# Gate sums on VectorE, denominators packed and their reciprocals spread by DMA, and the attention state folded into the output weights on 16 tiles of 32x32

## The chip, the core and the metric

The kernel runs on one core of a Trainium2 chip. The metric is the device time of one execution in microseconds (us). The core has a matrix engine (TensorE, "PE" in the profile; its weight loads are "PEld"), VectorE (DVE), ScalarE (ACT), GpSimd (POOL) and SyncE (SP), which here issues nearly all DMAs. In the traces here each engine works through its own queue in the order in which the kernel wrote it, and engines wait for each other on semaphores.

All runs below are of the same state (fast, granted TensorE clock 0.996 to 1.000). The runs came in five groups, each in turn on one chip, and the kernel before stood in each; its median moved between groups by 0.1 us only.

## The reference, cut to what matters

For `x` of 2048 tokens by 1024, two attention blocks with 32 heads of 32 are mixed by a gate. Block A is linear attention, block B a sliding window (not touched by the change, apart from its place in the schedule).

```python
g = sigmoid((x * gate_w).sum(-1, keepdims=True))
# block A
phi = lambda t: where(t > 0, t + 1, exp(t)) + 1e-6
pq, pk = phi(q), phi(k)
kv  = einsum("bhsd,bhse->bhde", pk, v)          # the state, 32x32 a head
z   = pk.sum over tokens                         # 32 numbers a head
den = einsum("bhqd,bhd->bhq", pq, z) + 1e-6      # one number a head and token
a   = ((pq @ kv) / den) @ A_wo
return g * a + (1 - g) * b
```

Both kernels fold the state into the weights: `(pq/den) @ (kv @ A_wo)`. So three small products stand beside the large ones: the gate sums, the denominators, and the fold of `kv` into `A_wo`.

## The kernel before: the parts that matter here

The kernel is written as a list of operations with costs. A scheduler inside it runs that list through a simple model of the engines ("the plan") and so fixes each engine's order; it then emits waits for what each operation reads.

The gate, on TensorE, with the sums on four column tiles, then a trip through DRAM to turn the layout:

```python
for dc in range(8):
    for u in range(4):
        last = e.matmul(gbank.ap()[32*u:32*u+32, :], gwr[:, dc, :], xT[:, dc, u*512:(u+1)*512],
                        start=(dc == 0), stop=(dc == 7), tile_position=(0, 32*u), ...)
P.op("act", lambda e: e.activation(gts[:, :], gbank.ap(), ACT.Exp, scale=-1.0), ...)
... # store gts, load it back transposed, 1/(1+.)
```

The state is placed as four 32x32 blocks on the diagonal of eight 128x128 matrices (`kvbd`), turned by TensorE, and folded with full matmuls; `zbd` repeats `z` so that a full matmul gives the denominator in every row of its head:

```python
def fold(i, jh):       # 16 of these
    P.op("pe", lambda e: e.matmul(bank.ap(), kvT[:, i, :], ws[1][:, i, jh*512:(jh+1)*512], start=True, stop=True), ...)
    move(ws[1][:, i, jh*512:(jh+1)*512], bank.ap, 512, bank, w)

def numer(u, j):       # 32 of these: queries of heads 4j..4j+3, tokens 512u..512u+511
    group(bank, w, xs, [wr, xr])                       # 8 full matmuls
    phi(bank, p_, preg, 8*u + j)                       # Exp on ACT, two operations on DVE
    def over():
        P.op("pe", lambda e: e.matmul(db.ap(), zbd[:, j, :], p_, start=True, stop=True), ..., name="den")
        P.op("act", ... R = Ln(den + eps))
        P.op("act", ... R = Exp(-R))                   # the reciprocal
        P.op("dve", lambda e: e.tensor_tensor(dst, p_, R[:, :], ALU.mult), ...)
    after(6 if u == 0 else 2, over)
```

The end of the program: all engines read a flag (whether the fast path's range assumptions held) and jump over a slower general path, which in all these runs is not taken. SyncE first waits for every DMA semaphore that the kernel used:

```python
def tail(e, eng):
    e.wait_ge(*flag_op.val)
    e.reg_load(reg, flag[0:1, 0:1])
    if eng == "sp":
        for s, v in P.final:              # one entry for each DMA semaphore
            e.wait_ge(s, v)
    with e.If_eq(reg, 0):
        ... # the general path
```

## Time and profile before

501.64 us, median of 3 runs (501.62 to 503.03).

| engine | busy, us | share of the span |
|---|---|---|
| PE | 493.2 | 99% |
| DVE | 267.6 | 54% |
| ACT | 191.4 | 38% |

From the profile page of the kernel before. In a group's line the columns are: source line, engine, operation, output and input tiles, shapes, count, busy us in total and mean ns of one, then the engine's idle time just ahead of them.

```profile
span 500.1 us, 11359 instructions
PE 493.2 (99%) x5113; PEld 231.4 (46%) x5113; DVE 267.6 (54%) x460; ACT 191.4 (38%) x331; POOL 6.6 (1%) x30
PE 96%; SPq 2%; DMA 1%; ACT 1%; issue 0%; DVE 0%
L1325 PE MATMUL ps_all<-w,xT 128*128 128x512 bf16 x960 | 214.2, 379 | 1.1 <-DMA xT<-in_A_x_dram 0.9
L1607 ACT ACTIVATE ra<-ps_all,eps 128x512 f32<-128x512 f32 x32 | 21.5, 689 | 2.1 <-PE ps_all L1605 2.0
```

The third line is the chain of work that ended last: 96% of it is TensorE. The 379 ns of one matmul is not what it costs, because matmuls overlap; the cost shows in the chain. From the chain of waits of the kernel before, in order of time (start us, us, what):

```profile
62.08 1.84 PE ps_all L1393 x32
128.55 5.29 PE ps_all L1325 x24
325.53 0.45 PE ps_all L1573 x8
327.70 0.86 PE ps_all L1583 x4
330.30 0.22 PE ps_all L1605
342.42 0.69 ACT ra L1607
343.11 0.58 ACT e L1334 x2
343.69 0.52 ACT ra L1608
344.20 1.17 ACT ra L1607 x2
```

Full matmuls (L1325) cost 5.29 / 24 = 0.22 us each, or 0.216 in long runs. L1393 is the gate, L1573 the turn, L1583 the fold, L1605 a denominator. The last four lines are the one place where TensorE depends on ACT.

### The profile page before, as it was taken

What the parts mean: (1) busy time and instruction counts of PE and PEld (TensorE: products, weight loads), DVE (VectorE), ACT (ScalarE), POOL (GpSimd) and SP (SyncE); (2) the same over time, 40 slices, a digit from 0 to 9 for tenths busy, and PEclk for the clock granted to TensorE, in tenths of its full rate; (3) what the DMA queues carried; (4) which work ended last, traced back from release to release, by engine and by line L of the source; (5) the groups of instructions that cost most, each with busy time, mean ns of one, the idle gap of its engine ahead of it and who ended that gap; (6) DMA issues with size and microseconds to landing.
All of it is one profiled execution on the core that took longest, in us unless ns stands there. A gap on an engine that the chain in (4) does not pass through costs nothing.

```text
span 500.1 us, 11359 instructions
## 1 busy us (share of the span) xinstructions
PE 493.2 (99%) x5113; PEld 231.4 (46%) x5113; DVE 267.6 (54%) x460; ACT 191.4 (38%) x331; POOL 6.6 (1%) x30
## 2 busy tenths in 40 slices
PE   8999999999999999999999999999999999999996
PEld 3444444444444445554545454444444444444443
DVE  3112136555676785665556564678776663234443
ACT  1111111111334345656655555489955543200000
POOL 5000000000000000000000000000000000000000
PEclk9999999999999999999999999999999999999999
DMA  8999990000023151011010000500000000011222
GB/s 230 202 209 312 344 283 1 1 0 1 12 90 125 32 182 34 24 42 26 27 43 24 24 1 3 171 0 1 0 2 0 1 1 0 3 43 64 84 85 67
DMA packets 47410, 34.91 MB, mean 70 GB/s; under 512 B 22261, under 2 KB 43125, under 8 KB 47354
## 3 DMA queue, kind: packets, MB, share of 16 engines
q1 hardware_dynamic: 46810, 33.59, 23.6%
q8 instruction: 42, 0.69, 0.6%
q10 hardware_dynamic: 544, 0.52, 0.4%
q14 instruction: 14, 0.11, 0.1%
HBM read 21.51 MB, written 8.40 MB: 60 GB/s over the span
## 4 chain that ended last, share of the span: by engine, by line
PE 96%; SPq 2%; DMA 1%; ACT 1%; issue 0%; DVE 0%
PE ps_all L1325 76%; PE ps_all L1680 11%; PE ps_all L1428 2%; PE ps_all L1447 2%; PE ps_all L1605 1%; SPq L1295 1%; PE ps_all L1526 1%; DMA w<-in_B_wqkv_dram 1%; PE ps_all L1454 1%; PE ps_all L1583 1%; SPq L1300 1%; ACT ra L1607 0%; PE ps_all L1393 0%; ACT e L1334 0%; ACT ra L1608 0%
## 5 line engine op out<-in xcount | busy, mean ns | idle before, releaser
L1325 PE MATMUL ps_all<-w,xT 128*128 128x512 bf16 x960 | 214.2, 379 | 1.1 <-DMA xT<-in_A_x_dram 0.9
L1325 PE MATMUL ps_all<-xT,w 128*128 128x512 bf16 x768 | 172.1, 379 | 0.1
L1325 PEld LDWEIGHTS ps_all<-w,xT 128*128 128x128 bf16 x960 | 91.1, 98 | 109.9 <-DMA w<-in_B_wqkv_dram 1.4
L1325 PEld LDWEIGHTS ps_all<-xT,w 128*128 128x128 bf16 x768 | 74.1, 98 | 88.8 <-ACT ra L1607 0.6
L1680 PE MATMUL ps_all<-w,qT 128*128 128x512 bf16 (+1 forms) x264 | 55.4, 373 | 0.0
L1680 PEld LDWEIGHTS ps_all<-w,qT 128*128 128x128 bf16 x264 | 25.8, 98 | 29.7
L1336 DVE TENSOR_SCALAR e<-e 128x512 bf16<-128x512 bf16 x64 | 18.4, 291 | 30.9 <-ACT e L1332 17.1
L1434 ACT ACTIVATE E<-ps_all 128x1824 bf16<-128x1824 f32 (+1 forms) x18 | 30.4, 1688 | 11.7 <-PE ps_all L1428 10.9
L1356 DVE CAST vst<-ps_all 128x512 bf16<-128x512 f32 x15 | 10.4, 692 | 42.7 <-PE ps_all L1325 42.7
L1437 DVE TENSOR_TENSOR E<-E,msk 128x1824 bf16<-128x1824 bf16 (+1 forms) x18 | 19.8, 1102 | 22.2 <-ACT E L1434 22.2
L1684 DVE SCALAR_TENSOR_TENSOR o<-ps_all,gm,xT 128x512 bf16<-128x512 f32 (+1 forms) x25 | 18.2, 729 | 23.0 <-PE ps_all L1680 22.8
L1334 ACT ACTIVATE e<-ps_all 128x512 bf16<-128x512 f32 x32 | 19.2, 601 | 27.5 <-PE ps_all L1325 26.0
L1332 ACT ACTIVATE e<-ps_all 128x512 bf16<-128x512 f32 x32 | 19.1, 598 | 26.7 <-PE ps_all L1325 25.8
L1281 DVE TENSOR_TENSOR mx<-mx,qT 128x1024 bf16<-128x1024 bf16 x32 | 20.7, 688 | 15.3 <-ACT qT L1360 15.2
L1281 DVE TENSOR_TENSOR mx<-mx,kT 128x1024 bf16<-128x1024 bf16 x32 | 20.7, 688 | 14.8 <-ACT kT L1357 14.7
L1357 ACT ACTIVATE vst<-ps_all 128x512 bf16<-128x512 f32 x17 | 10.2, 597 | 47.8 <-PE ps_all L1325 47.8
L1466 DVE TENSOR_TENSOR qT<-ps_all,L 128x456 bf16<-128x456 f32 (+1 forms) x36 | 21.0, 627 | 6.2 <-ACT L L1464 5.0
L1463 ACT ACTIVATE L<-ps_all 128x456 f32<-128x456 f32 (+1 forms) x36 | 17.8, 547 | 12.4 <-PE ps_all L1447 12.4
L1607 ACT ACTIVATE ra<-ps_all,eps 128x512 f32<-128x512 f32 x32 | 21.5, 689 | 2.1 <-PE ps_all L1605 2.0
L1338 DVE SCALAR_TENSOR_TENSOR pk<-ps_all,e 128x512 bf16<-128x512 f32 x32 | 21.9, 688 | 0.7
L1359 DVE TENSOR_SCALAR xT<-ps_all,g 128x512 bf16<-128x512 f32 x15 | 11.2, 750 | 19.9 <-PE ps_all L1325 19.9
L1360 ACT ACTIVATE qT<-ps_all 128x512 bf16<-128x512 f32 x14 | 8.4, 597 | 34.4 <-PE ps_all L1325 34.4
(77 smaller groups left out, 321.2 us busy)
## 6 DMA issues: line engine op xcount, KB each, us to landing
w<-in_A_wqkv_dram SPq DMA_DIRECT2D x6, 1024.0 KB, 7.0
v<-vB_hbm SPq DMA_DIRECT2D x36, 128.0 KB, 2.6
vB_hbm<-vst SPq DMA_DIRECT2D x32, 128.0 KB, 4.7
w<-in_B_wqkv_dram SPq DMA_DIRECT2D x4, 1024.0 KB, 8.4
out_dram<-o SPq DMA_DIRECT2D x15, 256.0 KB, 2.0
w<-in_A_wo_dram SPq DMA_DIRECT2D x2, 1024.0 KB, 5.2
w<-in_B_wo_dram SPq DMA_DIRECT2D x2, 1024.0 KB, 6.7
w<-in_B_wqkv_dram SPq DMA_DIRECT2D x6, 256.0 KB, 4.3
```

What stands on the lines that cost most here:

```text
L1281: P.op("dve", lambda e, m=m, op=op: e.tensor_tensor(m[:, 0:n], m[:, 0:n], src, op), 0.08 + n / 1920.0, reads=[m.all(), reg], writes=[m.all()],
L1325: last = e.matmul(bank.ap(), lhs(dc), rhs(dc), start=(dc == 0), stop=(dc == 7))
L1332: P.op("act", lambda e: e.activation(e_[:, :], bank.ap(), ACT.Exp), act(512), reads=[bank.iv], writes=[e_.all()])
L1334: P.op("act", lambda e: e.activation(e_[:, :], bank.ap(), ACT.Exp, accum_out=qe[:, col:col + 1]), act(512) + 0.1, reads=[bank.iv], writes= ...
L1336: P.op("dve", lambda e: e.tensor_scalar(e_[:, :], e_[:, :], 1.0, 1e-6, op0=ALU.min, op1=ALU.add), 0.25, reads=[e_.all()], writes=[e_.all()])
L1338: P.op("dve", lambda e: e.scalar_tensor_tensor(out=dst, in0=bank.ap(), scalar=0.0, in1=e_[:, :], op0=ALU.max, op1=ALU.add), dps(512), read ...
L1434: P.op("act", lambda e: e.activation(E[:, 0:32 * nq].rearrange("p (j q) -> p j q", j=4), ps[:, 4:8, 0:8 * nq], ACT.Exp), act(32 * nq), rea ...
L1437: P.op("dve", lambda e: e.tensor_tensor(ev(), ev(), m[:, :, :].rearrange("p r q -> p (r q)")[:, None, :].to_broadcast([128, 16, 2 * nq]), ...
L1466: P.op("dve", lambda e, L=L, h=h, q0=q0: e.tensor_tensor(qT[:, :, q0:q0 + nq], SO[h].ap(0, n).rearrange("p (c q) -> p c q", c=8), L[:, 0:n ...
L1607: P.op("act", lambda e: e.activation(R[:, :], db.ap(), ACT.Ln, bias=eps[:, :]), act(512), reads=[db.iv, eps.all()], writes=[R.all()])
L1680: last = e.matmul(bank.ap(0, f1 - f0), qT[:, dc, t * 128:(t + 1) * 128], ws[3][:, dc, f0:f1], start=(dc == 0), stop=(dc == 7))
L1684: P.op("dve", lambda e, bank=bank, o_=o_, t=t, n=n, i0=i0, i1=i1, tgt=tgt, c0=c0: e.scalar_tensor_tensor(out=o_[:, i0 * 128:i1 * 128].rear ...
```

## The change

Its intent is to take small work off TensorE, which bounds the kernel.

1. The gate's sums move to VectorE: x is loaded a second time in natural order, and one operation for each of 16 token tiles multiplies and sums.
2. The denominators of 8 head groups are made together: 8 matmuls on four column tiles ("a pack"), 4 packs in all. Each head's denominator is made once instead of in 32 rows, its reciprocal is taken once, and DMAs spread it over the rows (store to DRAM, load with a repeated row). The 32 reciprocal pairs on ACT become 4.
3. The fold runs as 4 packs of 16 matmuls of 32x32, four output banks each. The heads are laid out anew, so that a 32x32 transpose by VectorE replaces TensorE's turn.
4. Three output tiles of block B are moved ahead of the last part of block A, to cover the last spread.

The diff, cut to its core (the head layout, tile allocation and the moved final loop are left out):

```diff
-        P.op("pe", gate_fn, 1.75, mode="c", reads=[gwr.all(), xT.all()], writes=[gbank.iv], name="gate")
... (store and load of the gate)
+        for t in range(NT):
+            xt, xs_ = xn.next()
+            P.op("sp", lambda e, t=t, xt=xt: e.dma_start(xt[:, :], x2[t // 8, (t % 8) * 128:(t % 8) * 128 + 128, :]), ...)
+            P.op("dve", lambda e, t=t, xt=xt: e.scalar_tensor_tensor(out=xt[:, :], in0=xt[:, :], scalar=1.0, in1=gwb[:, :],
+                                                    op0=ALU.mult, op1=ALU.mult, accum_out=gt[:, t:t + 1]), ...)
... (fold)
-            P.op("pe", lambda e: e.matmul(bank.ap(), kvT[:, i, :], ws[1][:, i, jh * 512:(jh + 1) * 512], ...), name="fold")
+                for r in range(4):
+                    for c in range(4):
+                        sl = 4 * I + r
+                        last = e.matmul(four[c].ap()[32 * r:32 * r + 32, :], kvT[32 * c:32 * c + 32, 32 * sl:32 * sl + 32],
+                                        ws[1][32 * c:32 * c + 32, sl, jh * 512:(jh + 1) * 512], tile_position=(32 * c, 32 * r), ...)
... (denominators: now one call for each u, three slots after the last numerator of u)
+        def over(u):
+                for q in range(2):
+                    for c in range(4):
+                        last = e.matmul(db.ap()[32 * c:32 * c + 32, :], zsel[:, 2 * c + q, :], tgt[:, 2 * c + q, c0:c0 + 512],
+                                        start=(q == 0), stop=(q == 1), tile_position=(0, 32 * c), ...)
... (R = Exp(-Ln(den + eps)) on ACT as before)
+            for c in range(4):
+                P.op("sp", ... e.dma_start(rc_hbm[u, 8 * c:8 * c + 8, :, :], R[32 * c:32 * c + 8, None, :].to_broadcast([8, 4, 512])), ...
+                     chan="rco%d_%d" % (rs, c), lat=0.5)
+            for j in range(8):
+                B, bs = RBr.next()
+                src = rc_hbm[u, 4 * j:4 * j + 4, :, :].rearrange("r k n -> (r k) n")[:, None, :].to_broadcast([16, 8, 512])
+                P.op("sp", ... e.dma_start(B[:, :], src), ..., chan="rci%d" % bs, lat=1.0)
+                P.op("dve", ... e.tensor_tensor(dst, dst, B[:, :], ALU.mult), ...)
```

## The prediction

> **What bounds the kernel now.** TensorE, from about 8 us to 496 us. The page gives PE 99% of a 500.1 us span; the chain of waits is 96% PE; PE's list of waits has only start-up (1.3 us warm tile, 0.9 us xT); the granted clock is 1.00 in every stage window. In the chain 8 full matmuls (128x128 weights, 512 columns) cost 1.73 us, 0.216 us each. DVE is 54% and ACT 38% busy and matter only where they hold PSUM banks: in the numerator-and-fold stage (window 326 to 346 us: DVE 16.6, ACT 17.6 of 20 us) the chain turns to ACT for 3 us, and PE loses about 0.4 us.
>
> So a us off PE's queue should be a us off the time, if no new stall comes.
>
> **What the change takes off PE (times from the chain).**
> - Gate sums: 32 matmuls on four column tiles, 1.84 us, gone (DVE does them).
> - Turn: 8 transposes, 0.45 us, gone (one DVE transpose).
> - Denominators: 32 full matmuls x 0.216 = 6.9 us become 4 packs of 2 waves on four column tiles. The gate shows the price: 8 waves in 1.84 us. I estimate 0.54 a pack, 2.2 us. Saves 4.7.
> - Fold: 16 full matmuls, 3.45 us, become 4 packs of 16 tiles of 32x32. The Trainium skill (TensorE: Matmul & The Clock Gate, Part 3, measured speedup) gives 10.6x for 16 such tiles. This trace has only 8 at once: 8 sums of 456 columns took 0.19 us, and 64 small matmuls 0.63 us, about 10 ns each. Estimate for a pack: 0.216 + 16 x 0.01 + drain, about 0.45 us; 1.8 us in all. Saves 1.7.
> - The ACT-bound stall: 0.4 us.
>
> The Trainium skill (TensorEngine Tiling (Array Packing), Key Properties) says a change of tiling mode drains TensorE; here 24 full matmuls between tiled ones took 5.29 us where 24 x 0.216 is 5.18, so a visit costs about 0.1 us, counted above.
>
> Sum: 9.1 us, all on the critical path.
>
> **What it adds, off the path.** DVE: 16 products summed over 1024 columns, about 1.2 us each by the 0.69 us of a 512-column one, 19 us, in the query/key stage (DVE 34.6 of 64 us busy). ACT loses 28 pairs of Ln and Exp, 28 x 1.33 = 37 us. DMA: 4 MB of x and four spreads of 2.3 MB. A 1 MB load lands in 5 to 7 us, so a spread in about 10, its whole chain in about 15 us against 17 to 30 us of slack. The DMA queues are empty there (share 0.00 to 0.01). The x loads queue behind the weights, so the full DMA of the first 64 us (share 1.04) should not slow the start.
>
> **Prediction.** 501.64 - 9.1 = 492.5 us; range 491.2 to 495.0. Two per cent is 491.6, just beyond the centre: faster by over 2% 0.25, within 2% 0.71, slower 0.04.
>
> **What would show it.** PE stays 99% busy; full matmuls and the S, PV and state stages keep their times; in the chain a fold pack is about 0.45 us and a denominator pack 0.54; gate and turn are gone; ACT falls to about 155 us, DVE rises to about 285; no PE wait on the spread tiles.
>
> **What would make it wrong.** A spread that lands late, so that DVE, in order, waits for it and holds banks; folds that wait for four free banks (1.3 us of evictions each on DVE and ACT, every 3.5 us); 32x32 tiles less parallel than thought (four serial waves are 0.9 us a pack); x loads delaying the query/key weights; or cheaper packs, which would carry it past 2%.

## The result, and the profile after

495.38 us (median of 4 runs, 495.11 to 495.74), against 501.63 us before (501.51 to 503.03): 6.25 us less, where 9.1 were predicted, and 0.4 us above the top of the range. The ratio is 0.987 (95% interval 0.985 to 0.989). Ratios here are the mean time of one kernel's fast runs over that of the other's of the same rounds, so not quite the ratio of the medians.

From the profile page of the kernel after:

```profile
span 493.6 us, 11394 instructions
PE 477.7 (97%) x5055; PEld 226.2 (46%) x5121; DVE 274.7 (56%) x487; ACT 166.9 (34%) x287; POOL 5.1 (1%) x27
PE 89%; DMA 3%; SPq 3%; issue 2%; DVE 2%; ACT 1%; ACTq 0%
L1601 DVE TENSOR_TENSOR xT<-xT,rb 128x512 bf16<-128x512 bf16 x24 | 16.3, 689 | 8.7 <-DMA rb<-rc_hbm 8.5
```

TensorE has only 89% of the chain now: DMA, the DMA queue and DVE have come into it. (66 matmul records are missing from this trace, so that its PE count and its busy time are slightly low; the weight loads are all there. The 2% of "issue" are gaps that they leave: the profile of the same kernel taken again, e13, has all 5121 records, no such gaps, and PE with 98% busy and 87% of the chain.) In the last line, VectorE stands idle 8.5 us in all in front of multiplications, waiting for spread tiles. TensorE's own list of waits shows that one such wait reached it (line waited for, us, times, longest):

```profile
PE ps_all L1585 <- DVE xT L1326: 1.0, 1, 1.0
```

L1585 is a denominator pack, L1326 the last step of phi. The timeline of TensorE in the stage with the packs (start us, us, engine, line, operation, shapes, count, and in brackets the idle time ahead):

```profile
318.30 3.40 PE L1313 MATMUL ps_all<-xT,w 128*128 128x512 bf16 x15 [0.16 <-issue]
321.63 0.43 PE L1558 MATMUL ps_all<-w,kvT 32*32 32x512 bf16 x16
322.00 3.63 PE L1313 MATMUL ps_all<-xT,w 128*128 128x512 bf16 x16
325.68 0.44 PE L1558 MATMUL ps_all<-w,kvT 32*32 32x512 bf16 x16
...
335.73 0.62 PE L1585 MATMUL ps_all<-pq,zsel 128*32 128x512 bf16 x8
336.27 15.71 PE L1313 MATMUL ps_all<-xT,w 128*128 128x512 bf16 x71
...
368.08 1.89 PE L1313 MATMUL ps_all<-xT,w 128*128 128x512 bf16 x8
370.95 0.62 PE L1585 MATMUL ps_all<-xT,zsel 128*32 128x512 bf16 x8 [0.98 <-DVE xT L1326]
371.50 1.90 PE L1313 MATMUL ps_all<-w,pq 128*128 128x512 bf16 x8
```

The price of a pack is read from starts, because ends are modelled: from the end of the full matmuls ahead (their start plus 0.2158 us each) to the start of the next full one, which can be read to about 0.02 us. Fold packs: 0.46, 0.60, 0.46 and 0.48 us. Denominator packs: 0.64, 0.71, 1.69 and 0.64 us; the third holds the wait.

And the chain of waits of the kernel after, around that third pack:

```profile
354.04 3.31 DMA rc_hbm<-ra
...
362.60 6.98 DMA rb<-rc_hbm
369.60 0.69 DVE xT L1601
370.29 0.61 DVE xT L1326
370.95 0.62 PE ps_all L1585 x8
```

The spread's last tile lands at 369.58 us, 15.5 us after its first store was issued at 354.04. SyncE issues the four stores and eight loads one after another, so that the last load goes out only at 362.60, 8.6 us after the first store. Of that load's 16 parts 15 had landed by 368.04; the wait runs to the last one. VectorE multiplies with the tile, and only then does the phi that TensorE waits for.

**Where the 2.9 missing microseconds are.** The start of the last VectorE instruction is a good mark: 495.65 us before, 488.07 after, so 7.58 us are gained up to there. From that mark to the end of the profiled run (its own time: 501.81 and 495.56) it is 6.16 us before and 7.49 after. So of the 2.9 us, 1.5 were lost on TensorE and 1.3 after TensorE was done.

The end is best read from SyncE's own records (semaphore waits are not counted as busy and do not stand in the page). This is SyncE after its last store; "x26" is a run of wait instructions:

```
before  last store issued  496.66 to 497.09     after  last store issued  488.97 to 489.40
        load of the flag   497.15 to 497.65            load of the flag   489.46 to 489.96
        waits  x26         497.70 to 499.26            waits  x9          490.00 to 490.58
        branch             499.30 to 499.35            waits  x31         490.95 to 492.82
        end of its part    499.81                      branch             492.86 to 492.92
                                                       end of its part    493.36
```

The kernel before uses 53 DMA semaphores, the kernel after 81 (the spread alone adds 8 for its stores and 12 for its loads). The records show two semaphores to an instruction and about 61 ns an instruction. The walk through them takes 1.56 us before and 2.82 after; 0.37 us of the latter is the gap between its ninth and tenth instruction.

### The profile page after: what moved, and what is told of

Read it like the earlier page. It is cut to its first block, busy times and chain, and to the rows that moved or that the text cites. A ratio compares the mean times of both kernels' runs of the same rounds, so it can differ in the third digit from the quotient of the medians.

```text
span 493.6 us, 11394 instructions
## 1 busy us (share of the span) xinstructions
PE 477.7 (97%) x5055; PEld 226.2 (46%) x5121; DVE 274.7 (56%) x487; ACT 166.9 (34%) x287; POOL 5.1 (1%) x27
## 4 chain that ended last, share of the span: by engine, by line
PE 89%; DMA 3%; SPq 3%; issue 2%; DVE 2%; ACT 1%; ACTq 0%
PE ps_all L1313 71%; PE ps_all L1634 11%; PE ps_all L1405 2%; PE ps_all L1424 2%; DMA rb<-rc_hbm 1%; SPq L1287 1%; PE ps_all L1506 1%; SPq L1598 1%; DMA w<-in_B_wqkv_dram 1%; PE ps_all L1431 1%; DMA rc_hbm<-ra 1%; DVE zsel L1548 1%; SPq L1292 1%; DVE pq L1326 0%; PE ps_all L1585 0%
## 5 line engine op out<-in xcount | busy, mean ns | idle before, releaser
L1313 PE MATMUL ps_all<-w,xT 128*128 128x512 bf16 x921 | 207.5, 380 | 5.4 <-issue 4.3
L1313 PE MATMUL ps_all<-xT,w 128*128 128x512 bf16 x748 | 167.5, 379 | 2.3 <-issue 1.7
L1324 DVE TENSOR_SCALAR e<-e 128x512 bf16<-128x512 bf16 x64 | 18.3, 291 | 33.8 <-ACT e L1320 17.2
L1326 DVE SCALAR_TENSOR_TENSOR pk<-ps_all,e 128x512 bf16<-128x512 f32 x32 | 21.9, 688 | 0.7
L1345 ACT ACTIVATE kT<-ps_all 128x512 bf16<-128x512 f32 x16 | 9.6, 597 | 35.8 <-PE ps_all L1313 35.8
L1601 DVE TENSOR_TENSOR xT<-xT,rb 128x512 bf16<-128x512 bf16 x24 | 16.3, 689 | 8.7 <-DMA rb<-rc_hbm 8.5
L1348 ACT ACTIVATE qT<-ps_all 128x512 bf16<-128x512 f32 x16 | 9.6, 597 | 31.5 <-PE ps_all L1313 31.5
```

What stands on the lines that cost most here:

```text
L1313: last = e.matmul(bank.ap(), lhs(dc), rhs(dc), start=(dc == 0), stop=(dc == 7))
L1324: P.op("dve", lambda e: e.tensor_scalar(e_[:, :], e_[:, :], 1.0, 1e-6, op0=ALU.min, op1=ALU.add), 0.25, reads=[e_.all()], writes=[e_.all()])
L1326: P.op("dve", lambda e: e.scalar_tensor_tensor(out=dst, in0=bank.ap(), scalar=0.0, in1=e_[:, :], op0=ALU.max, op1=ALU.add), dps(512), read ...
L1345: fa = lambda e: e.activation(dst, src(), ACT.Copy)
```

## The experiments

Theories: **A**, the walk of SyncE is what makes the end longer (rival **B**: the landing of the last stores does). **C**, TensorE's wait at the third pack comes from a spread tile that lands late, in front of which VectorE, in order, holds up phi (rival **D**: VectorE has too much work, or the pack is planned too close). **E**, packs cost what their waves cost plus a fixed visit (rival **F**: the small tiles run partly one after another). **G**, the gate's cost was wholly on the path (rival **H**: its replacement gives some back). **J**, formed after e5 and e6: two things hold the end, and each alone is enough.

### e3_ready: multiplications that wait for no DMA (wrong values on purpose)

```diff
-e.tensor_tensor(dst, dst, B[:, :], ALU.mult)
+e.tensor_tensor(dst, dst, gwb[:, :].bitcast(F32), ALU.mult)     # a tile that is always there
 ...
+    for o in P.ops:
+        if o.name == "mul":
+            o.deps = {d for d in o.deps if d.chan is None}     # after the plan has fixed the order
```

> After kernel, same order of instructions on every engine and the same DMAs, but the 32 multiplications with the spread reciprocals read a tile that has long been there (wrong values on purpose) and so wait for no DMA. Theory C (PE's 0.98 us wait ahead of the third denominator pack is DVE standing in its queue before a reciprocal tile that lands late, which holds up the phi that the pack reads): the wait goes, time falls by about 1.0 us to 494.4. Rival D (DVE has too much work there, or the pack is just planned too close behind its phi): the wait stays, 495.4.

494.90 us (494.66 to 495.23). It was run at another time. TensorE's list of waits has no L1585 any more; what is left is the start-up:

```profile
PE ps_all L1352 <- DVE warm L1266: 1.3, 1, 1.3
PE ps_all L1313 <- DMA xT<-in_A_x_dram: 0.6, 1, 0.6
```

The DMAs and the multiplications are as before, so the amount of VectorE's work is not the cause (D falls), and C stands. The gain, 0.5 us, is smaller than the 1.0 expected. It is read from the trace and not from the totals: the intervals of the ratio to before overlap for the kernel after (0.9851 to 0.9888), e3 (0.9846 to 0.9876) and e4 (0.9845 to 0.9875). The wait differs from run to run: in seven profiles of kernels with the same spread and order of multiplications (after, e1, e5, e13, e14, e15, e16) its longest piece was 0.98, 0.45, 1.02, 0.25, 0.8, 0.2 and 0.5 us, 0.6 on the mean.

### e4_plan: a slower DMA in the kernel's own model

```diff
-chan="rco%d_%d" % (rs, c), lat=0.5)
+chan="rco%d_%d" % (rs, c), lat=1.0)
-chan="rci%d" % bs, lat=1.0)
+chan="rci%d" % bs, lat=1.2)
```

> After kernel with a slower DMA in the kernel's own planning model for the spread (0.5 to 1.0 us for a store, 1.0 to 1.2 us for a load, which puts the last load where the profile has it); the plan then orders VectorE's queue differently, TensorE's order, the work and the DMAs are the same. Theory C: the late tile no longer stands ahead of the phi, the 0.98 us wait goes, time about 494.4. Rival D: no gain, 495.4.

494.69 us (494.53 to 494.93), and correct. It was run at another time. TensorE's order is the same; VectorE's is not. The timeline of TensorE in this kernel at the third pack:

```profile
368.31 1.89 PE L1313 MATMUL ps_all<-xT,w 128*128 128x512 bf16 x8
370.13 0.62 PE L1585 MATMUL ps_all<-xT,zsel 128*32 128x512 bf16 x8
370.68 1.90 PE L1313 MATMUL ps_all<-w,pq 128*128 128x512 bf16 x8
```

No wait is left: the pack starts 0.1 us after the full matmuls end. And why, from the timelines of VectorE, first after, then in this kernel:

```profile
367.12 1.28 DVE L1601 TENSOR_TENSOR xT<-xT,rb 128x512 bf16<-128x512 bf16 x2
368.32 0.29 DVE L1324 TENSOR_SCALAR e<-e 128x512 bf16<-128x512 bf16 x1
369.60 0.69 DVE L1601 TENSOR_TENSOR xT<-xT,rb 128x512 bf16<-128x512 bf16 x1 [1.00 <-DMA rb<-rc_hbm]
370.21 0.68 DVE L1326 SCALAR_TENSOR_TENSOR xT<-ps_all,e 128x512 bf16<-128x512 f32 x1
```

```profile
367.51 0.29 DVE L1324 TENSOR_SCALAR e<-e 128x512 bf16<-128x512 bf16 x1 [0.52 <-ACT e L1322]
367.84 0.69 DVE L1326 SCALAR_TENSOR_TENSOR xT<-ps_all,e 128x512 bf16<-128x512 f32 x1
368.44 1.28 DVE L1601 TENSOR_TENSOR xT<-xT,rb 128x512 bf16<-128x512 bf16 x2
```

After: a multiplication (L1601) stands between the two steps of phi (L1324 and L1326), and is idle 1.00 us for its tile. In e4_plan the two steps stand together and the multiplications come behind. The DMAs and the work are the same, but for two evictions that the new plan moved from ScalarE to VectorE; the plan now has the last load land where the profile has it.

### e11_bf16: the reciprocals in bf16, half the bytes

```diff
-rc_hbm = nc.dram_tensor("rc_hbm", [4, H, 4, 512], F32)
+rc_hbm = nc.dram_tensor("rc_hbm", [4, H, 4, 512], BF16)
-e.activation(R[:, :], R[:, :], ACT.Exp, scale=-1.0)
+e.activation(Q[:, :], R[:, :], ACT.Exp, scale=-1.0)     # Q: bf16, likewise the tiles B
```

> After kernel with the reciprocals written, spread and multiplied as bf16 instead of fp32: half the bytes in the spread, the same number of DMAs, the kernel's plan has the same times. Theory C (late tiles, because of the bytes): the tiles land earlier, PE's 1 us wait before the third denominator pack goes, about 494.5. If the lateness is in issuing and latency and not in the bytes: the wait stays, 495.4. VectorE's multiplication may get faster, which frees only an engine off the path.

494.51 us (494.25 to 495.65), correct. A load lands 2.5 us after its issue, not 5.1, and TensorE's wait is gone. The last tile of the second spread lands 9.8 us after its first store, not 15.5, and 7.3 us of that are still issuing. So most of the lateness lies in the bytes. (In its profile the start was 1 us later than usual, waiting for xT.) A multiplication takes 0.42 us instead of 0.69, so this run changes two things; it is e3 that shows that VectorE's work is not the cause.

### e8_den_twice and e9_fold_twice: the price of a pack

```diff
-                for q in range(2):                 # e8: the waves of a denominator pack twice
+                for q in (0, 1, 0, 1):
-                for r in range(4):                 # e9: the 16 matmuls of a fold pack twice
+                for r in (0, 1, 2, 3, 0, 1, 2, 3):
```

> After kernel; each of the 4 denominator packs runs its two waves of four column tiles twice (same result, same order on every engine). Theory E (a pack costs 0.216 us a wave plus a fixed visit of about 0.21 us to the tiled mode, 0.64 in all): +4 x 2 x 0.216 = +1.73 us, 497.1. Rival F (the column tiles run partly one after another, 0.32 a wave): +2.6 us, 498.0.

> After kernel; each of the 4 fold packs runs its 16 matmuls of 32x32 tiles twice (same result, same order on every engine). Theory E (all 16 stream at once, so 16 more cost 0.216 us): +0.9 us, 496.3. Rival F (only 4 at a time): +3.5 us, 498.9.

e8: 497.85 us (497.49 to 498.39). e9: 495.31 us (494.89 to 495.50). They were run at other times. By the totals alone e8 would speak for F (498.0 expected), and e9 shows no cost at all. They show why a total should not be the only measure: the wait at the third pack moves along. In e8 the reciprocals start later, so the wait grew to 1.74 us, 0.76 more, which with 8 waves of 0.22 makes the 2.5 us measured; in e9 everything between the folds and the packs is later by 0.7 us, and the wait was 0 in its profile. The timelines are plain. e8, its first pack, and e9, its second fold pack:

```profile
335.90 1.05 PE L1585 MATMUL ps_all<-pq,zsel 128*32 128x512 bf16 x16
336.88 15.71 PE L1313 MATMUL ps_all<-xT,w 128*128 128x512 bf16 x71
```

```profile
325.90 0.65 PE L1558 MATMUL ps_all<-w,kvT 32*32 32x512 bf16 x32
326.48 3.63 PE L1313 MATMUL ps_all<-xT,w 128*128 128x512 bf16 x15
```

From the start of the pack to the next full matmul: 0.98 us for four waves against 0.54 for two (335.73 to 336.27 after), so 0.22 a wave. For the fold, 32 small matmuls take 0.58 us and 16 take 0.37 (321.63 to 322.00 after): 16 more cost 0.21 us, the time of one full matmul. All 16 tiles stream at once. E stands, F falls. What remains of a denominator pack, 0.64 - 2 x 0.216 = 0.21 us, is the visit: 0.1 us to get in (335.63 to 335.73) and 0.1 to get out.

### e10_gate_only: the gate part of the change alone, in the kernel before

```diff
-        P.op("pe", gate_fn, 1.75, mode="c", ...)       # and its store, load and tiles
+        for t in range(NT): ...                        # as in the change
```

> Before kernel with the gate part of the change alone: no gate matmuls, the gate's sums by VectorE from natural-order loads of x. Everything else as before (53 final semaphores). Theory G (the gate was wholly on the critical path and its replacement wholly off it): minus 1.84 us for the matmuls and about 0.1 to 0.2 for entering and leaving the tiled mode, 501.6 to 499.6. Rival H (the x loads or the VectorE products give some of it back in the projection stages): less than 1 us gained.

499.99 us (499.61 to 501.44) against 501.72 before: 1.7 us less, ratio 0.9963 (0.9945 to 0.9980; the mean of before holds two runs of 503.5). In the profile, the query and key stage starts at 61.96 us, and at 63.86 before. The two lines are from the timelines of TensorE, before and in this kernel (cut off where the query ended):

```profile
63.86 64.06 PE L1325 MATMUL ps_all<-xT,w 128*128 128x512 bf16 x296
61.96 8.37 PE L1325 MATMUL ps_all<-xT,w 128*128 128x512 bf16 x38
```

The stage keeps its length, 63.99 and 63.98 us to the first matmul of the next. G stands: nothing is given back there.

### e1_out_waits and e2_more_waits: the walk shortened after, lengthened before

```diff
-            for s, v in P.final:                            # e1: only the 4 semaphores of the output stores
+            for s, v in [(P.csem[c], n) for c, n in P.chan_n.items() if c.startswith("out")]:
-            for s, v in P.final:                            # e2, in the kernel before
+            for s, v in P.final + P.final[:28]:
```

> After kernel; at the end the SyncE queue waits only for the 4 semaphores of the output stores, not for all 81 DMA semaphores (the other 77 DMAs have readers that waited for them). Everything else is the same. In the profiles the time from the start of the last DVE instruction to the end of the span is 5.53 us after and 4.45 before. Theory A (the SyncE queue goes through one wait after another at about 0.04 us each; 28 more semaphores are the 1.08 us): the tail falls by 1.1 us or more, until the landing of the last store (about 3 us from its issue) bounds it; time 495.4 to about 494.0. Rival B (the tail is the landing of the last stores, or something in the output writes that differs): no change, 495.4.

> Before kernel with 28 of its 53 final semaphore waits written twice, so 81 waits as in the kernel after; nothing else changes. Theory A: the tail grows from 4.45 to about 5.5 us, time 501.6 to 502.7. Rival B: no change, 501.6.

e2: 503.33 us (503.27 to 503.44) against 501.72, so 1.6 us more, and the walk in its trace goes from 1.56 to 2.97 us. The walk does cost time. e1: 496.37 us (495.72 to 497.46): no gain, if anything slower. It was run at another time. Its trace shows SyncE branching at 490.95 us, 1.9 us earlier than after, but its next instruction starting only at 493.50; in the other kernels that takes 0.5 or 0.6 us. So A had its half right and was not enough. B falls: by the records of landings the last store had landed at 491.05 us in the kernel after, 1.8 us before its walk ended, and at 490.86 in e1.

### e5_hoist, e6_plan_hoist and e12_bf16_hoist: part of the walk moved to where SyncE is idle

```diff
+                if eng == "sp" and not hoisted and o.chan.startswith("out"):     # ahead of the first output store
+                    hoisted = True
+                    for s, v in [(self.csem[c], x) for c, x in chan_n.items()][:28]:
+                        e.wait_ge(s, v)
-            for s, v in P.final:
+            for s, v in P.final[28:]:
```

> After kernel; 28 of the 81 final semaphore waits of the SyncE queue stand ahead of the first output store, where that queue has idle time, so 53 are left at the end as in the kernel before. In the traces the queue walks these waits two to an instruction, 61 ns each: 26 instructions before (497.70 to 499.26 us), 40 after (490.00 to 492.82 us, with one gap of 0.37 us[...]). Theory A (the walk is what makes the tail longer; the kernel with 4 waits gained nothing only because its branch then waited 2.5 us for instructions): tail 4.5 us as before, time 495.4 to about 494.4. Rival B (the length of the walk doesn't matter): 495.4.

> e4_plan and e5_hoist together. Theories A and C: the two gains add, about 494.7 - 1.0 = 493.7. If they share a cause: 494.5.

> e11_bf16 and e5_hoist together. Theories A and C: 1 us less than e11_bf16, about 493.5, as e6_plan_hoist (492.9). If e5_hoist's lack of a gain is the rule: as e11_bf16.

e5: 495.64 us (495.21 to 496.25), no gain. It was run at another time. e12: 494.61 us (494.34 to 494.78), no gain over e11. e6: 492.93 us (492.83 to 493.34), 1.8 us better than e4_plan. In all three the walk is 26 instructions again. What went wrong in e5 and e12 shows in the single runs: the span is 1 us or more shorter, but the time of the run beyond the span is 2.9 to 3.2 us in e5 and 3.2 to 3.6 in e12, where it is 1.9 to 2.0 after and 1.7 in e6. So something else held the end as well. A first clue was that e6 has e4_plan's order, in which VectorE's queue has two instructions more: its final branch has 551 instructions ahead of it instead of 549. The trace also shows instruction fetches (packets of 8 KB) around the end. The 2.9 us between VectorE's branch (488.65 us after) and its next instruction (491.54) is no clue: that gap is 2.8 to 3.3 us in all 17 profiles, 3.1 before.

### e13_after: the kernel after once more, beside e10 to e12

> The kernel after, unchanged, on the same chip as the other three, for comparison with them: 495.4. All theories expect the third denominator pack to wait again for a phi that stands behind a late tile (0.98 us in the first profile; 0.45 to 1.74 us in the profiles of kernels with the same spread), and a tail of 5.5 us.

495.07 us (494.73 to 495.81). The wait was 0.25 us in this profile, the end 7.7 us.

### e14_dve_pad, e15_act_pad and e16_walk_dve_pad: the position of the final branch

```diff
+        if eng == "dve":                    # e14: e5_hoist with this;  e16: the kernel after with this
+            for t in range(4):              # e15: e5_hoist with eng == "act"
+                e.wait_ge(P.csem["x%d" % t], 16)     # met since the start
         e.wait_ge(*flag_op.val)
```

> e5_hoist with 4 semaphore waits more (2 instructions; all four were met long before) at the end of VectorE's queue, so that its final branch is instruction 551 as in e6_plan_hoist. Theory J (after the last stores two things run side by side, SyncE's walk and instruction fetches whose number depends on where the code of an engine ends; each alone holds the end at about 7.3 us, and both must go): the time beyond the span falls from 3.1 to 1.7 us, 495.6 to about 494.3. Rival K (the position of VectorE's code doesn't matter): 495.6.

> e5_hoist with the same 4 waits at the end of ScalarE's queue instead. If VectorE's position is what counts: 495.6 as e5_hoist. If ScalarE's is: about 494.3.

> The kernel after (long walk) with the 4 waits at the end of VectorE's queue. Theory J: the walk alone still holds the end, as in e4_plan: 7.3 us from the start of the last VectorE instruction, time 495.0 to 495.3; the time beyond the span 1.75 us instead of 1.92. Rival (the position alone is the cause): about 494.2.

e14: 493.87 us (493.49 to 494.56). e15: 494.89 us (494.73 to 495.20). e16: 495.40 us (494.57 to 496.71). Runs of other chips and other waits lie in these totals, so the end is compared by itself, from the start of the last VectorE instruction to the end of the profiled run, and by the time beyond the span in all runs:

| kernel | walk, instructions | instructions ahead of VectorE's branch | last VectorE start to run's end, us | beyond the span, us |
|---|---|---|---|---|
| before | 26 | 520 | 6.16 | 1.7 to 1.8 |
| e2_more_waits | 40 | 520 | 7.62 | 1.7 to 1.8 |
| e10_gate_only | 26 | 548 | 6.23 | 1.7 to 1.8 |
| after, e13 | 40 | 549 | 7.49, 7.74 | 1.8 to 2.1 |
| e4_plan | 40 | 551 | 7.28 | 1.7 to 1.8 |
| e16_walk_dve_pad | 40 | 551 | 7.52 | 1.7 to 1.9 |
| e5_hoist | 26 | 549 | 7.29 | 2.9 to 3.2 |
| e12_bf16_hoist | 26 | 549 | 7.59 | 3.2 to 3.6 |
| e15_act_pad | 26 | 549 | 7.58 | 2.7 to 3.3 |
| e6_plan_hoist | 26 | 551 | 6.19 | 1.7 |
| e14_dve_pad | 26 | 551 | 6.19 | 1.7 to 1.8 |

This is a two by two table, and J stands: with the long walk, or with VectorE's code ending where it does in the kernel after, the end is 7.3 to 7.7 us (7.9 in e1 and e3, whose branch has 549 ahead too); only without both is it 6.2, as before. With 520, 548 or 551 instructions ahead of the branch the short walk ends early; only 549 was ever seen to hold it. Two instructions that do nothing, placed in VectorE's queue, took the end from 7.3 (e5) to 6.2 us, and the same two in ScalarE's left it at 7.6. The records of DMA packets show what goes with it: from the last VectorE start on, all nine profiles with 549 and a walk of 26 or 40 have one instruction fetch of 8 KB more than those with 551 and the same walk. The last one starts 6.5 us or more after that mark, when no instruction is recorded any more (in e5 it ends at 7.00 us, the run at 7.29; in e14 the last fetch ends at 5.30, the run at 6.19). The kernel before has a late fetch too, but it ends at 5.99 us. That this fetch is what holds the end is an inference from that, and no record says for which engine it is, or why two instructions do away with it. That part stays open.

## Why the prediction was wrong

The mechanism was right: TensorE bound the kernel at full clock, the four small jobs were all on its path, and removing them shortened it with no new work becoming the bound. The sum was too large.

| term | predicted gain, us | measured, us | how |
|---|---|---|---|
| gate | 1.84 | 1.7 to 2.1 | e10; start of the next stage, 63.86 against 61.80 us |
| turn | 0.45 | 0.45 | gone |
| fold | 1.7 | 1.45 | 3.45 less packs of 0.46 + 0.60 + 0.46 + 0.48 |
| denominators | 4.7 | 3.2 | 6.91 less packs of 0.64 + 0.71 + 1.69 + 0.64 |
| stall on ACT | 0.4 | 0.4 | before, the matmuls at 343.01 and 345.42 us start 0.15 and 0.24 us late |
| the end | 0 | -1.3 | 6.16 against 7.49 us |
| sum | 9.1 | 6.25 | medians |

**The step that failed first: "a spread in about 10, its whole chain in about 15 us against 17 to 30 us of slack", and from it "no PE wait on the spread tiles".** Both sides of this comparison were off. The spread took 15.5 us from the first store's issue to the last landing where about 10 were predicted, and from the start of its denominator pack (351.98 us) to the landing (369.58) it was 17.6 where about 15 were predicted for the whole chain. And the deadline was nearer than the 17 us at the low end of the slack. That slack was meant to the first reader of the result, the output projection (the text does not say to what). The real deadline was set by VectorE's queue: the multiplications stand in it among phi's steps, and phi feeds the next denominator pack. Without its wait of 0.98 us the third pack would have started at 369.97 us; with the multiplication and phi's step ahead of it (0.69 and 0.61 us) the tile had to land by about 368.6, an estimate, which is 16.6 us after the start of the second pack. Taking away the DMA wait (e3), making the DMA slower in the plan (e4) and halving the bytes (e11) each removed TensorE's wait; mean times fell by about 0.5 to 0.7 us, which fits the wait of 0.2 to 1.0 us in the profiles. The prediction named this as a thing that could go wrong ("DVE, in order, waits for it"), and did not charge for it.

**The pack's price, 0.54 predicted, 0.64 to 0.71 measured without the wait.** The gate's line in the chain, 1.84 us, was taken as the whole price of a visit to the tiled mode. It leaves out the 0.1 us between the last full matmul and the first tiled one. Four packs make 0.4 to 0.5 us. The Trainium skill (TensorEngine Tiling (Array Packing), Key Properties) says that changing the tiling mode drains TensorE, and gives no time; here it is about 0.1 us each way. The fold's parallelism was as the Trainium skill (TensorE: Matmul & The Clock Gate, Part 3) has it for 16 tiles: e9 shows 16 more matmuls in 0.21 us, where one after another they would take 16 x 0.216 = 3.45. Its pack was 0.01 to 0.03 us dearer than estimated, and the second one started about 0.12 us late, for its banks as is likely (no list of waits shows it), which also was named as a risk.

**The end, 1.3 us, was not in the sum at all.** The prediction counted DMAs by bytes and landing, and not the semaphores that they bring: 28 more, walked at 61 ns for two (0.85 us, and the gap of 0.37) by an engine that had nothing else to do, after TensorE had ended. And beside it lay a second cost of the same size, which comes and goes with where VectorE's code ends, and which hid the gain of every attempt at the first until both were removed.

Two side forecasts missed as well: ACT fell to 166.9 us and not to 155, and DVE rose to 274.7 and not to 285. Evictions may go to either engine, and the plan gave more of them to ACT once it had room (55.8 us of them on ACT after the change against 48.0 before, 59.4 against 69.5 on VectorE).

The best version found is e6_plan_hoist: 492.93 us, correct, ratio to before 0.983 (0.981 to 0.984), against 0.987 of the kernel after. It is the change with two numbers in its plan raised until the last load lands where the profile has it, and 28 waits moved. It lies near the predicted 492.5, because it takes away most of what the prediction had left out.

## What to carry to other kernels

When work leaves a saturated engine for a DMA, the deadline of the landing is not the reader of the result but the first thing that stands behind the waiting instruction in an in-order queue; look at what that is, and give the plan measured DMA times. In this kernel every DMA semaphore was also a wait at the end: put those waits where their engine is idle and not behind the last store. When removing a cost from the end gains nothing, look for a second one beside it before dropping the theory, and test the two together.

## What the Trainium skill lacked or had wrong

- TensorEngine Tiling (Array Packing), Key Properties: that a change of tiling mode drains TensorE has no time with it. Here it is about 0.1 us in and 0.1 us out, 0.21 us for a denominator pack (0.64 us for two waves of 0.216).
- TensorE: Matmul & The Clock Gate, Part 3: the 10.6x for 16 tiles is given with 660 ns as the predicted time of the pack. Between full matmuls in a warm stream a pack of 16 with 512 columns took 0.37 us from its first start to the next full one, and 16 more in the same visit 0.21 us.
- Runtime: NRT & Kernel Launch, Instruction fetch mechanics: it says that a taken branch to code outside the window must wait for a fetch, and gives no time for the fetch. VectorE's jump over an untaken path took 2.8 to 3.3 us to its next instruction in all profiles here, and SyncE's 0.5 us, or 2.5 us in e1_out_waits. That two instructions more or less in a queue can be worth 1.1 us or more at the end of a run (7.29 and 7.58 against 6.19) is on no page.
- No page that I found gives the price of walking through semaphore waits that are already met: 61 ns an instruction with two semaphores, 2.8 us for 81 of them, 0.37 of it a gap.
